# High parts of operand sums moved from GpSimd to ScalarE in an attention and expert kernel

## The chip, the cores and the metric

The kernel runs on one core of one Trainium2 chip. The metric is the device time of one execution in microseconds (us), the median over several runs. The core has five engines that work from instruction streams of their own, each strictly in its own order: TensorE (PE) multiplies matrices, VectorE (DVE), ScalarE (ACT) and GpSimd (POOL) work elementwise, and SyncE (SP) issues the transfers between the chip's memory (DRAM) and the on-chip buffer (SBUF). They wait for each other by semaphores. Matrix products land in PSUM, of which this kernel uses banks of 128 x 512 numbers.

## The reference

First a causal attention with a decay bias over 32 heads of 576 positions and head size 64, then a layer of 4 experts on all 2304 tokens, weighted by given probabilities:

```python
scores = scale * np.matmul(q, k.transpose(0, 1, 3, 2))
cum = np.cumsum(np.maximum(s, 0.0), axis=-1)
bias = -(cum[:, :, :, None] - cum[:, :, None, :])
scores = np.where(causal, -1000000000.0, scores + np.minimum(bias, 0.0))
attn = softmax(scores)                       # rows sum to 1 (+1e-9)
x = np.matmul(attn, v)                       # then reshaped to 2304 x 512
p = domain_probs / (domain_probs.sum(-1, keepdims=True) + 1e-09)
for e in range(4):                           # w1: 512 x 1024, w2: 1024 x 512
    out += p[:, e:e + 1] * (np.maximum(x @ w1[e], 0.0) @ w2[e])
```

## The kernel before

Every factor of a product is held as two numbers, a high part (the value rounded to fp32r) and a low part (the value less its high part). A product is the sum of three matrix products: high by high, high by low, low by high.

**Two stages.** A planner (class `Sched`) orders the attention and, between its steps, a part of expert 0. It ends at some 280 us. What is left of expert 0 is written out in program order (the list `prog`), in groups of token tiles. Three groups are left: group 4 (tiles 10 and 11, 256 columns), group 5 (tiles 12 to 14, 384 columns) and group 6 (tiles 15 to 17, 384 columns). Each has a first layer (L942: `mo` or `pb` from `xg` and `w1h`, `w1l`), whose PSUM results ScalarE turns into the high part of the ReLU (L945, into `hT0`) and VectorE into the low part (L948, into `hT1`); and a second layer (L957), four output rows `dt` of 24 or, in groups 5 and 6, 12 matmuls each. A row `dt` takes first the high parts `hT0`, then the low parts `hT1`, then `hT0` again with `w2l`. VectorE multiplies its result by the token's probability into the sum `acc` (L1212). A group's input tile `xg` is a single buffer: it can be fetched (L932) only when the first layer of the group before is through. Groups 5 and 6 take 48 matmuls for each layer.

From some 372 us on the other experts (and half of expert 0's hidden units) are computed by 2 x 2 block products in seven instead of eight multiplications (`first_layer`, `second_layer`, all matmuls at L1288). That needs sums and differences of blocks of the operands.

**The sums.** The tokens form three pairs of blocks, worked on in the order 1, 2, 0. For each pair `sums_of` makes four operands, called 5, 7, 6 and 3, each 128 x 768: a sum or difference on GpSimd (L1063), its high part on GpSimd (L465), its low part on GpSimd (L450). They are stored to DRAM (`xs_d`, L1096) from a ring of seven buffers (`x`). Pairs 1 and 2 start from single sums fetched from `xf_d` (L1079); pair 0 fetches the high and low parts (L1052) and first joins them on GpSimd (four additions, L1063), and its operands also stay in SBUF.

**The weights' sums.** VectorE makes sums of the blocks of `w1` (four additions of 128 x 512 from SBUF to SBUF, L1063, tiles `t2`, `w1r`, `t`) and of `w2` (four more, tiles `hx`, `w2r`); then ScalarE makes high parts and VectorE low parts of them (L450, tiles `w1l`, `w2l`).

**Fetching back.** The results of groups 0 to 2 were stored to `o_d` in the attention. `back` (L1199) fetches them into `acc`, in 20 transfers.

**What sets the order.** All of that is placed between the matmuls of `prog` by a table: each step has a due time, and after each matmul the steps are written out whose due time is at most `spent`, the sum of the matmuls' planned times. Due times only set the order of the instructions on each engine; nothing starts by the clock. On SyncE each transfer waits besides for the one issued eight before it.

Of the kernel before, what the change touches and what calls it, by code (L numbers as in the profile page):

```python
# [33 lines left out]
HALVES = [(e, s) for e in range(1, E) for s in range(2)] + [(0, 0)]  # L34
LONE = len(HALVES) - 1
LG = 2
SUM_AT = {1: ((0.3, 0.6, 0.9, 1.2), 2.0, 13.5), 2: ((6.0, 6.5, 16.0, 18.0), 23.0, 32.0), 0: ((31.0, 31.5, 32.0, 36.0), 42.0, 57.0)}
T_RAW = (20.0, 25.0)
T_W1 = 42.0
T_W2 = 50.0  # L40
T_BACK = 48.0
START = {7: "4"}
EARLY = {1: "1", 6: "s5", 5: "s7", 7: "2", 3: "s6", 4: "4"}
REST = {1: "6 5", 6: "s3 7", 5: "3"}
ALL = {1: "1", 2: "2", 6: "6", 5: "5", 7: "7"}
# [287 lines left out]
def body(ctx, tc, qk, qkv0, vp, s, dp, w1, w1s, w2, w2s, out):  # L333
# [115 lines left out]
    def sub(e, out, in0, in1):  # L449
        (nc.gpsimd if e == "POOL" else nc.vector).tensor_tensor(out=out, in0=in0, in1=in1, op=ALU.subtract)  # L450
# [572 lines left out]
    xpool = ctx.enter_context(tc.tile_pool(name="xring", bufs=7))  # L1023
    tpool = ctx.enter_context(tc.tile_pool(name="temps", bufs=6))
    spool = ctx.enter_context(tc.tile_pool(name="stage", bufs=1))
    acc = [[mpool.tile([P, TG], F32, name=f"acc{dt}_{b_}") for b_ in range(NT // TG)] for dt in range(KD)]

    def blocks_of(n0, n1):
        return [(b_, max(n0, TG * b_), min(n1, TG * b_ + TG)) for b_ in range(NT // TG) if max(n0, TG * b_) < min(n1, TG * b_ + TG)]
# [10 lines left out]
    def x_tile():  # L1040
        return xpool.tile([P, 2, 2, TG], F32R, tag="x", name="x")

    def temp():
        return tpool.tile([P, 2, TG], F32, tag="t", name="t")

    def flat4(t):
        return t.rearrange("p l k n -> p (l k) n").bitcast(F32)

    def load_block(t, g, i, j):

        n0 = PAIRS[g][i][0] * P
        nc.sync.dma_start(out=flat4(t), in_=xrd[j, :, :, n0:n0 + TG])  # L1052
# [9 lines left out]
    def add(e, out, in0, in1, op):  # L1062
        (nc.gpsimd if e == "POOL" else nc.vector).tensor_tensor(out=out, in0=in0, in1=in1, op=op)  # L1063

    def sums_of(g, held):

        raw, blocks = {}, {}  # L1070
        order = ((1, 0), (1, 1), (0, 0), (0, 1))

        def load(part):
            if held is not None and not held:
                held.update({o: x_tile() for o in (3, 4, 1, 2, 5, 7, 6)})
            for i, j in part:
                if held is None:
                    raw[i, j] = temp()
                    nc.sync.dma_start(out=raw[i, j], in_=xfr[g][j, :, :, TG * i:TG * i + TG])  # L1079
                else:  # L1080
                    t = held[{(0, 0): 1, (0, 1): 2, (1, 1): 4, (1, 0): 3}[i, j]]
                    load_block(t, g, i, j)
                    blocks[i, j] = t

        def join(i, j):
            raw[i, j] = temp()
            add("POOL", raw[i, j], blocks[i, j][:, 0].bitcast(F32), blocks[i, j][:, 1].bitcast(F32), ALU.add)

        def split(o, d, a_, b_, op):
            add("POOL", raw[d], raw[a_], raw[b_], op)  # L1090
            blocks[o] = held[o] if held is not None else x_tile()
            hi("POOL", blocks[o][:, 0], raw[d])
            sub("POOL", blocks[o][:, 1], raw[d], blocks[o][:, 0].bitcast(F32))

        def store(o):
            nc.sync.dma_start(out=xsv[g, SUMS[o]], in_=flat4(blocks[o]))  # L1096

        loads, now, out_at = SUM_AT[g]
        for at, part in zip(loads, order):
            yield at, lambda part=part: load((part,))  # L1100
        if held is not None:
            for i, j in order:
                yield now, lambda i=i, j=j: join(i, j)
                now += 1.9
        for o, d, a_, b_, op in ((5, (1, 1), (1, 0), (1, 1), ALU.add), (7, (1, 0), (0, 0), (1, 0), ALU.subtract),
                                 (6, (0, 0), (1, 1), (0, 0), ALU.subtract), (3, (0, 1), (0, 1), (0, 0), ALU.subtract)):
            yield now, lambda o=o, d=d, a_=a_, b_=b_, op=op: split(o, d, a_, b_, op)
            yield max(now, out_at), lambda o=o: store(o)
            now += 4.7
            out_at += 4.7  # L1110
# [105 lines left out]
    held = {}  # L1216
# [16 lines left out]
    for i, x in enumerate(prog):
        if x[0] == "load":
            if x[2].done is None:
                load_x(x[1], x[3])
        elif x[0] == "l1":
            if x[4].done is None:
                l1_mm(x[1], x[2], bank(x[5]), x[3], x[3] + UN)
                spent += UN * t_pe(x[2]) / 1e3  # L1240
        elif x[0] == "l1e":
            if x[3].done is None:
                l1_hi(x[1], x[2], bank(x[5]))
            if x[4].done is None:
                l1_lo(x[1], x[2], bank(x[5]))
        elif x[0] == "l2":
            if x[3].done is None:
                l2_mm(x[1], x[5], bank(x[4]), x[2], x[2] + UN, x[6])
                spent += UN * t_pe(x[5]) / 1e3
        else:  # L1250
            gi, dt = x[1]
            n0, n1 = GROUPS0[gi][0] * P, GROUPS0[gi][-1] * P + P
            if x[2].done is None:
                evict0(gi, dt, bank(x[4]))
            else:
                if x[3].done is None:
                    nc.sync.dma_start(out=o_d[dt * P:(dt + 1) * P, n0:n1], in_=tok["osb", x[1]][:, 0:n1 - n0])
                assert None not in spilled
                spilled.append((dt, n0, n1))
        if x[0] in ("l1", "l2"):  # L1260
            while steps and steps[0][0] <= spent:
                steps.pop(0)[3]()
        if i == last_l1:
            assert len(w1_first) == len(w2_first) == 3
            wsteps = w1_first
        if i >= last_l1 and wsteps and x[0] in ("l1e", "l2e"):
            for _ in range(3):
                if wsteps:
                    wsteps.pop(0)()
# [251 lines left out]
```

## Time and profile before

| quantity | value |
|---|---|
| median of 3 runs | 934.11 us (932.44 to 936.62) |
| the profiled execution | 933.43 us, span 931.7 us |
| PE busy | 911.6 us, 98% of the span |
| DVE busy | 704.3 us, 76% |
| POOL busy | 516.4 us, 55% |
| ACT busy | 491.9 us, 53% |
| DMA queue of SyncE | 67.1% of 16 engines' span |

PE is busy in nine tenths or more of each of the 40 slices of the page, save the fifteenth (326 to 349 us) and the last; the granted clock is below full in the fifteenth and sixteenth (326 to 373 us):

```profile
PE   9999999999999959999999999999999999999998
PEclk9999999999999988999999999999999999999999
```

So a time is read by asking where PE does not work, or works at a lower clock, and what it waits for there. Transfers issued by SyncE stand as SPq. An instruction's line number is that of the code above.

### The profile page before, as it was taken

Reading aid. Unit: us, or ns where it says so; the run is one execution under the profiler, and the core shown is the slowest. Engines: PE = TensorE matmul, PEld = TensorE weight load, DVE = VectorE, ACT = ScalarE, POOL = GpSimd, SP = SyncE. Lnnn points to the kernel's source line nnn. Section 1 sums busy time; section 2 is a strip of 40 time slices with the busy share of each in tenths; the row PEclk is TensorE's granted clock in tenths of the full one; section 3 lists DMA queues with packets and bytes.
Section 4 is the critical chain, followed back from the end, with each engine's and each line's share of the span. In section 5 each row is a group of like instructions: output and inputs, shape, how many; then the busy total and the mean of one; then the engine's idle time right before and its main releaser. Section 6 shows DMA issues by size and latency. Waiting matters only on the chain.

```text
span 931.7 us, 16516 instructions
## 1 busy us (share of the span) xinstructions
PE 911.6 (98%) x5566; PEld 882.4 (95%) x5566; DVE 704.3 (76%) x1599; ACT 491.9 (53%) x1117; POOL 516.4 (55%) x540
## 2 busy tenths in 40 slices
PE   9999999999999959999999999999999999999998
PEld 7789999899999958999999999999999999999998
DVE  7878888887861546687787878788778886788786
ACT  6898999998860111424443344353344424443343
POOL 4688887887735975017541644353447236541755
PEclk9999999999999988999999999999999999999999
DMA  6788888878517985987766587657864677667101
GB/s 166 190 251 244 229 226 226 237 204 254 169 57 243 376 282 186 312 304 254 231 208 219 196 299 226 206 174 248 299 220 157 223 254 255 217 197 253 61 26 68
DMA packets 132239, 201.34 MB, mean 216 GB/s; under 512 B 11496, under 2 KB 107820, under 8 KB 132156
## 3 DMA queue, kind: packets, MB, share of 16 engines
q1 hardware_dynamic: 132156, 200.30, 67.1%
q8 instruction: 44, 0.72, 0.3%
q14 instruction: 39, 0.32, 0.1%
HBM read 157.34 MB, written 29.05 MB: 200 GB/s over the span
## 4 chain that ended last, share of the span: by engine, by line
PE 88%; DVE 4%; ACT 2%; DMA 2%; SPq 2%; issue 1%; POOL 1%; ACTq 0%; POOLq 0%; DVEq 0%
PE pb L1288 49%; PE mo L1288 8%; PE mo L942 7%; PE mo L957 5%; PE pv L841 5%; PE T L791 3%; PE S L745 3%; PE S L742 2%; PE pb L957 1%; PE pb L942 1%; PE X L791 1%; DMA xs_d<-x 1%; SPq L1199 1%; ACT a L764 1%; DMA xg<-x_d 1%
## 5 line engine op out<-in xcount | busy, mean ns | idle before, releaser
L1288 PE MATMUL pb<-x,w1h 128*128 128x384 f32 x1064 | 270.7, 335 | 0.0
L1288 PEld LDWEIGHTS pb<-x,w1h 128*128 128x128 f32 x1064 | 191.4, 188 | 2.0 <-ACT t L1321 1.6
L1288 PE MATMUL pb<-x,w1l 128*128 128x384 f32 x532 | 177.8, 334 | 0.0
L1296 ACT ACTIVATE pb<-pb 128x384 f32<-128x384 f32 x112 | 53.1, 475 | 202.5 <-DVE t L1328 112.1
L450 POOL TENSOR_TENSOR hT_r<-t,hT_r 128x768 fp32r<-128x768 f32 x18 | 34.8, 1935 | 176.6 <-PE pb L1288 128.7
L1288 PE MATMUL pb<-hT_r,w2h 128*128 128x384 f32 x432 | 109.6, 334 | 0.0
L1288 PEld LDWEIGHTS pb<-x,w1l 128*128 128x128 f32 x532 | 99.8, 188 | 0.0
L942 PE MATMUL mo<-xg,w1h 128*128 128x384 f32 (+1 forms) x304 | 81.4, 338 | 11.5 <-DMA xg<-x_d 11.5
L463 ACT ACTIVATE hT_r<-t 128x768 fp32r<-128x768 f32 x76 | 64.1, 843 | 47.2 <-PE pb L1288 44.3
L764 ACT ACTIVATE a<-a,mx 128x576 f32<-128x576 f32 (+4 forms) x136 | 81.0, 598 | 13.1 <-DVE mx L756 10.2
L1411 DVE TENSOR_TENSOR acc<-pb,acc 128x384 f32<-128x384 f32 x152 | 78.8, 550 | 10.1 <-ACT pb L1296 6.5
L1288 PEld LDWEIGHTS pb<-hT_r,w2h 128*128 128x128 f32 x432 | 78.0, 188 | 0.0
L458 POOL TENSOR_SCALAR a<-a,sm 128x576 f32<-128x576 f32 (+5 forms) x111 | 60.6, 552 | 28.5 <-DVE sm L772 15.0
L450 DVE TENSOR_TENSOR hT_r<-t,hT_r 128x768 fp32r<-128x768 f32 x58 | 58.8, 1013 | 23.0 <-ACT hT_r L463 22.5
L1288 PE MATMUL pb<-xg,w2h 128*128 128x384 f32 x288 | 73.3, 335 | 1.0 <-ACT pb L1296 1.0
L1288 PE MATMUL pb<-hT_r,w2l 128*128 128x384 f32 x216 | 72.2, 334 | 0.0
L1328 DVE TENSOR_TENSOR t<-pb,t 128x384 f32<-128x384 f32 x78 | 39.8, 552 | 41.9 <-ACT t L1321 29.1
L942 PEld LDWEIGHTS mo<-xg,w1h 128*128 128x128 f32 x304 | 53.9, 197 | 14.1 <-DMA xg<-x_d 12.8
L1063 DVE TENSOR_TENSOR t<-t 128x768 f32<-128x768 f32 (+1 forms) x42 | 63.4, 1517 | 0.1
L450 POOL TENSOR_TENSOR xg<-t,xg 128x768 fp32r<-128x768 f32 x19 | 42.9, 2259 | 35.1 <-ACT xg L463 35.1
L820 DVE TENSOR_TENSOR aTl<-T,aTh 128x256 fp32r<-128x256 f32 (+2 forms) x103 | 51.3, 508 | 4.9 <-ACT aTh L463 3.7
L756 DVE CUSTOM_DVE_ANT_0 a<-S,mask 128x448 f32<-128x448 f32 (+4 forms) x107 | 48.1, 456 | 7.4 <-PE S L742 5.8
(245 smaller groups left out, 2335.5 us busy)
## 6 DMA issues: line engine op xcount, KB each, us to landing
x<-xs_d SPq DMA_DIRECT2D x68, 768.0 KB
x<-x_d SPq DMA_DIRECT2D x55, 768.0 KB
xs_d<-x SPq DMA_DIRECT2D x12, 768.0 KB
osb<-p_d SPq DMA_DIRECT2D x19, 384.0 KB
w1r<-in_w1s_dram SPq DMA_DIRECT2D x7, 1024.0 KB
w2r<-in_w2s_dram SPq DMA_DIRECT2D x7, 1024.0 KB
KK<-AB_r SPq DMA_DIRECT2D x24, 288.0 KB
xg<-x_d SPq DMA_DIRECT2D x16, 384.0 KB
```

What stands on the lines that cost most here:

```text
L450: (nc.gpsimd if e == "POOL" else nc.vector).tensor_tensor(out=out, in0=in0, in1=in1, op=ALU.subtract)
L458: (nc.gpsimd if e == "POOL" else nc.vector).tensor_scalar(out, in_, scale, 1.0 if bias is None else bias, op0=ALU.mult, op1=ALU.mult if bi ...
L463: nc.scalar.activation(out, in_, AF.Copy)
L756: nc.vector.tensor_tensor_reduce(out=z[0:n, j0:j1], in0=tok["S", (c, pi)][0:n, 0:j1 - j0], in1=mask[0:n, 448 - a + j0:448 - a + j1], scale ...
L764: nc.scalar.activation(z[0:n, 0:bb], z[0:n, 0:bb], AF.Exp, bias=tok["mx", c][0:n, k:k + 1], scale=-1.0, accum_out=tok["sm", c][0:n])
L820: nc.vector.tensor_tensor(out=dst, in0=src, in1=h_.bitcast(F32), op=ALU.subtract)
L942: nc.tensor.matmul(t[:, 0:w], wl[q][:, dc, o:o + P], xgt[:, l, dc, 0:w], start=(u == 0), stop=(u == 3 * KD - 1))
L957: nc.tensor.matmul(t[:, 0:w], wl[fc // 2][:, fc % 2, 128 * dt:128 * dt + 128], ht[:, fc, 0:w], start=(u == 0), stop=(u == 3 * len(fcs) - 1))
L1063: (nc.gpsimd if e == "POOL" else nc.vector).tensor_tensor(out=out, in0=in0, in1=in1, op=op)
L1288: nc.tensor.matmul(ts[u], wv[wl][:, k, 128 * u:128 * u + 128], x[xl_][:, k, :], start=start and k == 0 and n == 0, stop=k == 1 and n == 2, ...
L1296: nc.scalar.activation(out[u], in_[u], AF.Copy)
L1411: nc.vector.tensor_tensor(out=d, in0=ts[u], in1=d, op=ALU.add)
```

## The change

The constants that set the order change; in `sums_of` the three steps of an operand (sum, high, low) become separate steps with due times of their own, and the high part is made by ScalarE instead of GpSimd; the ring's buffers are taken with the fetches; the fetches of `xg` become steps with a due time 2.5 after their place; `back` fetches all four `dt` of a block at once (5 transfers instead of 20) and is due at 21 instead of 48; `acc` becomes one tile for each block of tokens; the steps that sum the weights are due at 32 and 37 instead of 36 and 50; in the table `FIRST` one operand's step moves by one product.

```diff
-SUM_AT = {1: ((0.3, 0.6, 0.9, 1.2), 2.0, 13.5), 2: ((6.0, 6.5, 16.0, 18.0), 23.0, 32.0), 0: ((31.0, 31.5, 32.0, 36.0), 42.0, 57.0)}
-T_RAW = (20.0, 25.0)
+SUM_AT = {1: ((0.3, 0.6, 0.9, 1.2), 15.0), 2: ((6.0, 6.5, 25.0, 25.5), 30.0), 0: ((33.0, 36.0, 38.5, 43.0), 45.0)}
+T_RAW = (20.0, 28.0)
-T_BACK = 48.0
+T_SUMS = (32.0, 37.0)
+T_BACK = 21.0
+T_XG = 2.5
-FIRST = {1: "s5 s7 1", 6: "s6 6", 5: "2 s3", 4: "5", 3: "7 3"}
+FIRST = {1: "s5 s7 1", 6: "s6 6", 5: "2 s3", 3: "5 7 3"}
...
-    acc = [[mpool.tile([P, TG], F32, name=f"acc{dt}_{b_}") for b_ in range(NT // TG)] for dt in range(KD)]
+    acct = [mpool.tile([P, KD, TG], F32, name=f"acc{b_}") for b_ in range(NT // TG)]
+    acc = [[t[:, dt] for t in acct] for dt in range(KD)]
...
-        def split(o, d, a_, b_, op):
+        def total(o):
+            d, a_, b_, op = sums[o]
             add("POOL", raw[d], raw[a_], raw[b_], op)
-            blocks[o] = held[o] if held is not None else x_tile()
-            hi("POOL", blocks[o][:, 0], raw[d])
-            sub("POOL", blocks[o][:, 1], raw[d], blocks[o][:, 0].bitcast(F32))
+
+        def high(o):
+            hi("ACT", outs[o][:, 0], raw[sums[o][0]])
+
+        def low(o):
+            sub("POOL", outs[o][:, 1], raw[sums[o][0]], outs[o][:, 0].bitcast(F32))
...
+        for at, f, o in ((0.0, total, 5), (0.0, total, 7), (2.6, high, 5), (2.6, low, 5), (2.6, total, 6), (4.6, high, 7), (4.6, low, 7),
+                         (4.6, total, 3), (8.6, high, 6), (8.6, low, 6), (12.4, high, 3), (12.4, low, 3),
+                         (8.5, store, 5), (12.0, store, 7), (15.7, store, 6), (18.0, store, 3)):
+            yield now + at, lambda f=f, o=o: f(o)
...
-        for dt, n0, n1 in spilled:
+        for n0, n1 in sorted({x[1:] for x in spilled}):
...
-                nc.sync.dma_start(out=acc[dt][b_][:, u0 - TG * b_:u1 - TG * b_], in_=o_d[dt * P:(dt + 1) * P, u0:u1])
+                nc.sync.dma_start(out=acct[b_][:, 0:len(ds), u0 - TG * b_:u1 - TG * b_],
+                                  in_=o_d[0:P * len(ds), u0:u1].rearrange("(d p) n -> p d n", p=P))
...
-    steps.append((T_W1 - 6.0, 9, 0, lambda: w_begin(1, w1_first)))
+    steps.append((T_SUMS[0], 9, 0, lambda: w_begin(1, w1_first)))
...
-    steps.append((T_W2, 9, 0, lambda: w_begin(2, w2_first)))
+    steps.append((T_SUMS[1], 9, 0, lambda: w_begin(2, w2_first)))
...
         if x[0] == "load":
             if x[2].done is None:
-                load_x(x[1], x[3])
+                steps.append((spent + T_XG, -1, x[3], lambda x=x: load_x(x[1], x[3])))
+                steps.sort(key=lambda x: x[:3])
```

How the instructions stand before and after is seen in three places. The first is VectorE, from the first product of group 4's second layer on (`acc` from `mo_102`); `t`, `w1r` are sums of `w1`, `hx`, `w2r` sums of `w2`. Before:

```order
L1212 TENSOR_TENSOR acc_3_3940<-mo_102,osb 128x256
L1212 TENSOR_TENSOR acc_3_3946<-mo_103,osb 128x256
L1063 TENSOR_TENSOR t_4330<-w1r 128x512
L1063 TENSOR_TENSOR w1r<-w1r 128x512
L1063 TENSOR_TENSOR t<-w1r,t_4330 128x512
L1063 TENSOR_TENSOR t<-w1r,t 128x512
L1212 TENSOR_TENSOR acc_3_3952<-pb_3965,osb 128x256
L1212 TENSOR_TENSOR acc_3_3958<-pb_3966,osb 128x256
L948 SCALAR_TENSOR_TENSOR hT_r<-pb_3967,hT_r 128x384
L450 TENSOR_TENSOR w1l_80<-w1r,w1h_76 128x512 x2
L948 SCALAR_TENSOR_TENSOR hT_r<-pb_3968,hT_r 128x384
L450 TENSOR_TENSOR w1l_81<-t,w1h_77 128x512
```

And with the change:

```order
L1224 TENSOR_TENSOR acc_3940<-mo_102,osb 128x256
L1066 TENSOR_TENSOR t_4264<-w1r 128x512
L1066 TENSOR_TENSOR w1r<-w1r 128x512
L1066 TENSOR_TENSOR t<-w1r,t_4264 128x512
L1066 TENSOR_TENSOR t<-w1r,t 128x512
L1224 TENSOR_TENSOR acc_3940<-mo_103,osb 128x256
L1066 TENSOR_TENSOR hx_f<-w2r 128x512
L1066 TENSOR_TENSOR w2r<-w2r 128x512
L1066 TENSOR_TENSOR hx_f<-hx_f,w2r 128x512
L1066 TENSOR_TENSOR hx_f<-w2r,hx_f 128x512
L1224 TENSOR_TENSOR acc_3940<-pb_3947,osb 128x256
L1224 TENSOR_TENSOR acc_3940<-pb_3948,osb 128x256
```

The four sums of `w1` now stand ahead of the second product of group 4 (`mo_103`), and the four sums of `w2`, which stood behind group 5's last low part, stand ahead of the third and fourth (`pb_3947`, `pb_3948`). All eight are thus ahead of the low parts of group 5's ReLU, which stand behind these rows, in the same order as before among the `w1l`.

The second place is SyncE's queue around the fetch of group 6's input (`xg`, 384 columns). Before, behind the stores of pair 2:

```order
L1199 DMA acc_1_3950<-o_d 128x256
L1199 DMA acc_2_3951<-o_d 128x128
L1199 DMA acc_1_3956<-o_d 128x256
L1199 DMA acc_2_3957<-o_d 128x128
L932 DMA xg<-x_d 128x2x384 x4
L1033 DMA osb<-p_d 128x384
L1096 DMA xs_d<-x 128x4x384 x3
L1033 DMA osb<-p_d 128x384
L1096 DMA xs_d<-x 128x4x384
```

And with the change:

```order
L1055 DMA x<-x_d 128x4x384
L1103 DMA xs_d<-x 128x4x384
L1055 DMA x<-x_d 128x4x384 x2
L1103 DMA xs_d<-x 128x4x384 x2
L1055 DMA x<-x_d 128x4x384
L1103 DMA xs_d<-x 128x4x384 x2
L1036 DMA osb<-p_d 128x384
L934 DMA xg<-x_d 128x2x384 x4
L1103 DMA xs_d<-x 128x4x384 x2
L1036 DMA osb<-p_d 128x384
L1103 DMA xs_d<-x 128x4x384 x2
```

The fetches of `acc` are gone from here (they stand, five in number, ahead of the first store). Ahead of `xg` stand the last stores of pair 2, mixed with the fetches of pair 0, and the fetch of probabilities `osb`.

The third place is ScalarE from group 4's sixth ReLU on; names carry buffer numbers here, `hT0_r_593` is written by the ReLUs and `w1h` from `w1r` and `t`. Before:

```order
L945 ACTIVATE hT0_r_593<-pb1_3966 128x256
L945 ACTIVATE hT0_r_593<-pb2_3967 128x256
L945 ACTIVATE hT0_r_593<-pb3_3968 128x256
L945 ACTIVATE hT0_r_593<-pb2_3967 128x384
L463 ACTIVATE w1h0_76<-w1r_4149 128x512 x2
L945 ACTIVATE hT0_r_593<-pb3_3968 128x384
L463 ACTIVATE w1h1_77<-t_4332 128x512
L945 ACTIVATE hT0_r_593<-mo_0_102 128x384
```

And with the change, where `x_3960` is the high part of pair 1's operand 3, and `x_4010` to `x_4013` are those of pair 2's operands 5, 7, 6 and 3:

```order
L947 ACTIVATE hT0_r_593<-pb1_3948 128x256
L947 ACTIVATE hT0_r_593<-pb2_3949 128x256
L465 ACTIVATE x_3960<-t_3972 128x768
L947 ACTIVATE hT0_r_593<-pb3_3950 128x256
L465 ACTIVATE x_4010<-t_4019 128x768
L465 ACTIVATE x_4011<-t_4014 128x768
L465 ACTIVATE x_4012<-t_4182 128x768
L947 ACTIVATE hT0_r_593<-pb2_3949 128x384
L465 ACTIVATE w1h0_76<-w1r_4125 128x512
L465 ACTIVATE x_4013<-t_4191 128x768
L465 ACTIVATE w1h0_76<-w1r_4125 128x512
L947 ACTIVATE hT0_r_593<-pb3_3950 128x384
```

High parts that wait for GpSimd's sums now stand between the ReLUs that wait for PE. The one of pair 1's operand 3 stands behind the seventh ReLU of group 4, and the last of pair 2 ahead of group 5's second ReLU.

## Rows read from the trace of the kernel before

**Rows 1.** Busy time of the engines by stretch: start:end, length, then each engine.
```profile
319.73:329.67 9.94, 9.22 (x50) 8.26 (x49) 7.18 (x10) 3.56 (x7) 5.80 (x4) 1.00 1.07 384
329.67:338.57 8.90, 8.78 (x49) 8.14 (x48) 6.81 (x5) 2.68 (x5) 7.50 (x4) 1.00 0.85 298
338.57:349.25 10.68, 0.01 (x2) 0.01 (x1) 0.00 (x0) 0.00 (x0) 10.42 (x8) 0.60 0.77 228
349.25:362.36 13.11, 12.27 (x48) 11.34 (x49) 8.35 (x8) 1.48 (x3) 12.32 (x8) 0.67 0.81 274
362.36:371.87 9.51, 9.35 (x50) 8.44 (x50) 5.44 (x11) 2.05 (x4) 0.00 (x0) 1.00 0.23 83
```

**Rows 2.** Chain that ended last: start, length, engine, tile, line, instructions.
```profile
280.22 8.32 PE mo L957 x48
```

**Rows 3.** SyncE's DMA queue in order of time: start, length, line, transfer, count.
```profile
323.50 11.42 SPq L1096 DMA_DIRECT2D xs_d<-x  x3
334.97 10.40 SPq L1199 DMA_DIRECT2D acc<-o_d  x20
345.47 1.91 SPq L932 DMA_DIRECT2D xg<-x_d  x4
```

**Rows 4.** TensorE in order of time: start, length, operands, count, idle before.
```profile
329.67 1.95 PE L957 MATMUL pb<-hT_r,w2h 128*128 128x384 f32 x8
349.25 1.01 PE L942 MATMUL mo<-xg,w1h 128*128 128x384 f32 x2 [10.67 <-DMA xg<-x_d]
353.48 1.01 PE L942 MATMUL mo<-xg,w1h 128*128 128x384 f32 x2 [0.84 <-DMA xg<-x_d]
```

**Rows 5.** Granted TensorE clock in stretches of 2 us (the fourth number, PEclk).
```profile
342.00:344.00 2.00, 0.00 (x0) 0.50 0.67 178
356.00:358.00 2.00, 2.00 (x8) 0.53 0.93 338
358.00:360.00 2.00, 2.00 (x14) 1.00 0.82 285
```

**Rows 6.** GpSimd in order of time, the second and third pair's sums.
```profile
313.14 1.85 POOL L1063 TENSOR_TENSOR t<-t 128x768 f32<-128x768 f32 x1
315.08 1.16 POOL L465 TENSOR_SCALAR x<-t 128x768 fp32r<-128x768 f32 x1
316.32 2.16 POOL L450 TENSOR_TENSOR x<-t,x 128x768 fp32r<-128x768 f32 x1
318.44 2.29 POOL L1063 TENSOR_TENSOR t<-t 128x768 f32<-128x768 f32 x1
330.98 1.32 POOL L465 TENSOR_SCALAR x<-t 128x768 fp32r<-128x768 f32 x1 [5.29 <-DMA xs_d<-x]
```

**Rows 7.** VectorE in order of time, 311 to 330 us.
```profile
311.29 0.42 DVE L1212 TENSOR_TENSOR acc<-mo,osb 128x256 f32<-128x256 f32 x1 [1.98 <-PE mo L957]
314.51 1.03 DVE L1063 TENSOR_TENSOR t<-w1r 128x512 f32<-128x512 f32 x1
315.57 1.20 DVE L1063 TENSOR_TENSOR w1r<-w1r 128x512 f32<-128x512 f32 x1
316.69 4.58 DVE L1063 TENSOR_TENSOR t<-w1r,t 128x512 f32<-128x512 f32 x2
321.20 0.74 DVE L1212 TENSOR_TENSOR acc<-pb,osb 128x256 f32<-128x256 f32 x2
326.77 0.55 DVE L948 SCALAR_TENSOR_TENSOR hT_r<-pb,hT_r 128x384 fp32r<-128x384 f32 x1
328.89 0.69 DVE L450 TENSOR_TENSOR w1l<-w1r,w1h 128x512 fp32r<-128x512 f32 x1
```

**Rows 8.** ScalarE in order of time: a ReLU, and a high part of 768.
```profile
307.03 0.39 ACT L945 ACTIVATE hT_r<-pb 128x256 fp32r<-128x256 f32 x1 [1.12 <-PE pb L942]
394.01 0.83 ACT L463 ACTIVATE hT_r<-t 128x768 fp32r<-128x768 f32 x1
```

**Rows 9.** Chain that ended last: the landing of a store of sums.
```profile
319.17 11.66 DMA xs_d<-x
```

More of the change, by code (lines that the diff above doesn't have):

```diff
@@ L1065, in sums_of, with load @@
     def sums_of(g, held):
-        raw, blocks = {}, {}
+        raw = {}
         order = ((1, 0), (1, 1), (0, 0), (0, 1))
[L1073 to L1083, printed above, removed]
+        def load(i, j):
+            if not outs:
+                outs.update({o: x_tile() for o in ((5, 7, 6, 3) if held is None else (3, 4, 1, 2, 5, 7, 6))})
+                if held is not None:
+                    held.update(outs)
+            if held is None:
+                raw[i, j] = temp()
+                nc.sync.dma_start(out=raw[i, j], in_=xfr[g][j, :, :, TG * i:TG * i + TG])
+            else:
+                load_block(outs[whole[i, j]], g, i, j)
@@ L1085, in join @@
         def join(i, j):
             raw[i, j] = temp()
-            add("POOL", raw[i, j], blocks[i, j][:, 0].bitcast(F32), blocks[i, j][:, 1].bitcast(F32), ALU.add)
-        def split(o, d, a_, b_, op):
+            t = outs[whole[i, j]]
+            add("POOL", raw[i, j], t[:, 0].bitcast(F32), t[:, 1].bitcast(F32), ALU.add)
+        def total(o):
+            d, a_, b_, op = sums[o]
             add("POOL", raw[d], raw[a_], raw[b_], op)
-            blocks[o] = held[o] if held is not None else x_tile()
-            hi("POOL", blocks[o][:, 0], raw[d])
-            sub("POOL", blocks[o][:, 1], raw[d], blocks[o][:, 0].bitcast(F32))
+        def high(o):
+            hi("ACT", outs[o][:, 0], raw[sums[o][0]])
@@ L1095, in store @@
+        def low(o):
+            sub("POOL", outs[o][:, 1], raw[sums[o][0]], outs[o][:, 0].bitcast(F32))
         def store(o):
[L1096 to L1100, printed above, removed]
-        if held is not None:
[L1102 to L1110, printed above, removed]
+            nc.sync.dma_start(out=xsv[g, SUMS[o]], in_=flat4(outs[o]))
@@ new lines, in sums_of @@
+        outs = {}
+        whole = {(0, 0): 1, (0, 1): 2, (1, 1): 4, (1, 0): 3}
+        sums = {5: ((1, 1), (1, 0), (1, 1), ALU.add), 7: ((1, 0), (0, 0), (1, 0), ALU.subtract),
+                6: ((0, 0), (1, 1), (0, 0), ALU.subtract), 3: ((0, 1), (0, 1), (0, 0), ALU.subtract)}
+        loads, now = SUM_AT[g]
+        for at, (i, j) in zip(loads, order):
+            yield at, lambda i=i, j=j: load(i, j)
+        if held is not None:
+            for k, (i, j) in enumerate(order):
+                yield now + 1.9 * k, lambda i=i, j=j: join(i, j)
+            now += 7.6
@@ L1196, in back @@
     def back():
-        for dt, n0, n1 in spilled:
+        for n0, n1 in sorted({x[1:] for x in spilled}):
+            ds = [dt for dt, *x in spilled if x == [n0, n1]]
+            assert ds == list(range(len(ds)))
             for b_, u0, u1 in blocks_of(n0, n1):
-                nc.sync.dma_start(out=acc[dt][b_][:, u0 - TG * b_:u1 - TG * b_], in_=o_d[dt * P:(dt + 1) * P, u0:u1])
+                nc.sync.dma_start(out=acct[b_][:, 0:len(ds), u0 - TG * b_:u1 - TG * b_],
+                                  in_=o_d[0:P * len(ds), u0:u1].rearrange("(d p) n -> p d n", p=P))
         spilled.append(None)
```

## The prediction

> **What bounds the kernel now.** I read the page's slices first: PE is busy nearly everywhere, so only a stretch in which it waits can give time back. Cutting that stretch at the ends of layers [rows 1] shows groups 5 and 6. Each of the four layers has 48 matmuls, which take 8.32 us where nothing disturbs them [rows 2], so four take 33.3; from 319.73 to 371.87 they take 52.14. The loss of 18.9 us is the most that the change can give in this stretch: 9.94 - 8.32 = 1.6 in group 5's first layer, 8.90 - 8.32 = 0.6 in its second, 10.7 idle, 13.11 - 8.32 = 4.8 in group 6's first, 1.2 in its second [rows 1]. Then the queue and PE in order of time: PE waits 10.67 us for group 6's `xg` [rows 4], and SyncE reaches that fetch at 345.47 only, because three stores that wait for GpSimd hold it for 11.42 us and the 20 fetches of `acc` for 10.40 more [rows 3]. Last the clock: it stands at 0.50 within the idle time, is at 0.53 in the 2 us before 358 and at 1.00 after [rows 5]. Of the 4.8 us in group 6's first layer 0.84 is a second wait [rows 4]; the rest, 3.95, I put down to that lower level (1.2 instead of 2.4 GHz).
>
> **The queue's part.** With `acc` fetched earlier and in five pieces, 10.40 us leave SyncE's queue ahead of `xg`. The five come ahead of the first store, where SyncE has to wait for GpSimd. One piece is not in the trace: between 0.48 us (1.91 for four `xg`) and 3.8 (11.42 for three stores, waits included) [rows 3]; I take 0.52, the mean of the old ones, 2.6 in all. At 19 us, the upper end, the cover would be used up but `xg` of group 5 still waits for PE to free its buffer at about 308.
>
> What is left ahead of group 6's `xg` are pair 2's last stores. They need pair 2's last low part. GpSimd now runs eight additions for a pair, without the four high parts (0.83 us for one on ScalarE, [rows 8]). But it starts pair 2 no earlier: ScalarE makes pair 1's last high part only behind group 4's seventh ReLU (307.03 + 0.39, [rows 8]), which PE's progress fixes, so the high part ends at 308.3 and the low part, 1.85 us [rows 6], at 310.1. From there pair 2's eight additions take 8 x 1.85 = 14.8 alone and 8 x 2.29 = 18.3 beside VectorE (below), and end at 325 to 328.5. The old pause of 5.29 us, in which GpSimd waited for a buffer [rows 6], goes. So `xg` is issued once group 5's first layer frees it, at 328 to 331, and lands within the 11.66 us that the slowest store in this stretch took [rows 9], by 342. For the queue alone, PE would lose 0 to 4 us there instead of 10.7.
>
> **What is late next: VectorE.** The eight sums of the weights now stand ahead of two results of group 4, and of the low parts of group 5's ReLU. Such a sum from SBUF to SBUF takes 0.69 us at 328.89, in GpSimd's pause before 330.98 [rows 6, 7]. While GpSimd works it is another thing. GpSimd's instructions end at 314.99, 316.24, 318.48 and 320.73 [rows 6]; the four sums of `w1` end at 315.54, 316.77, 318.98 (the mean of the two) and 321.27 [rows 7]. Each ends 0.50 to 0.55 us after a GpSimd instruction, and the next GpSimd instruction ends later by as much. So the two take turns, one sum for one addition; where GpSimd only adds, a turn is 4.58 / 2 = 2.29 us. Instructions that read PSUM are not held up: a low part takes 0.55, a pair of results 0.74 [rows 7].
>
> The rule behind it is in the Trainium skill, SBUF — State Buffer, section "Who interferes with whom": a VectorE instruction with two SBUF inputs and a GpSimd instruction that reads SBUF exclude each other, and the second one waits until the first is through. By that rule a sum would end its full 0.69 after GpSimd's end; the trace shows 0.50 to 0.55. With 0.69 the twelve turns below would be 0.15 to 0.2 longer each and the forecast some 2 us higher; I go by the row.
>
> Now the turns, with GpSimd busy without a pause (pair 2's eight additions, then pair 0's joins):
> - VectorE is through with group 4's first result at 311.29 + 0.42 = 311.7 [rows 7]. GpSimd's first addition of pair 2 ends at 312.0, the first sum of `w1` at 312.5.
> - Seven more turns for the other seven sums: 312.5 + 7 x 2.29 = 328.5. (The second result of group 4 stands among them and costs no turn.)
> - The last two results of group 4: 0.74, 329.2. Group 5's second layer, ready at 319.73 + 8.32 = 328.05, needs the first of these banks.
> - First low part 0.55, then two `w1l` (turns 9 and 10, 330.8 and 333.1), second low part 333.6, `w1l` 335.4, third 335.9, `w1l` 337.7, fourth low part 338.2.
>
> PE has done four matmuls with high parts by then, and one for each low part that came. From the last low part on, 137 are left: 5 of this row, 36 of the other three, 96 of group 6. At 8.32 / 48 they take 23.75 us. PE was all but idle for 8 us, so I charge the lower clock as the trace shows it after 10.67 us idle, 3.95, and 0.6 for group 6's second layer, as group 5's lost (its first eight matmuls took 1.95, [rows 4]). End: 338.2 + 23.75 + 3.95 + 0.6 = 366.5, against 371.87. Group 6's `xg` (by 342) is then no longer waited for, since group 5 ends at about 348.
>
> **The rest at nothing.** The second stage gets the same instructions; pair 0's sums, with twelve additions and some four turns behind 328.5, end near 355, ahead of its first use after 366. The step moved in `FIRST` is one high and one low part that VectorE has 6 us to make (three products of 12 matmuls) before their product. The tile `acc` in another shape moves no work. A waiting high part on ScalarE holds up the ReLUs behind it: pair 2's last one follows a sum that ends at about 323.5, the ReLU behind it is ready at 323.9 (half of group 5's first layer), so about 1 us, hidden behind VectorE.
>
> **Sum.** 371.87 - 366.5 = 5.4 us less. The profiled execution took 933.43 (span 931.7), so 928.0; the median of the runs shown is 0.7 above it, 928.7 from there. I take 928.4. The forecast's own range: with the lower clock not granted at all 924.5; with one turn more (2.29) and 0.8 us more behind ScalarE 931.5.
>
> **Rivals.**
> A. The eight sums fit in. If GpSimd pauses in pair 2 (a high part that comes late, a buffer not yet free), sums run in 0.69 instead of 2.29, and all twelve end by about 321 and the low parts with their ReLUs. Then PE runs 319.73 + 33.3 + 0.6 = 353.6 plus 0 to 4 for `xg`: 14 to 18 us less, 916 to 920; with some turns left 922. For it: GpSimd now depends on ScalarE for each low part, and paused 5.29 us in this place before. Against: by the sums above every high part is ready before its turn.
> B. ScalarE holds PE. The high part of pair 2's operand 3 needs the buffer of a store issued at about 312; the slowest landing was 11.66 us [rows 9], so 324, with no room left. Each us after that moves three of group 5's ReLUs; landing at T, the last low part comes at about T + 4, which passes 338.2 at T = 334, and the gain is gone at 339.5: 934. Against: twice the slowest landing.
> C. The clock stays low. At 0.50 each of the 137 matmuls costs 0.173 more. The sum holds 3.95, some 23 of them. If new waits break PE's work (group 6's results and low parts behind `w2l`, which take turns with pair 0 too) and the level stays, the gain is used up after 54 matmuls, it is slower by 0.5% after about 81, and at all 137 the end is 338.2 + 47.5 + 0.6 = 386.3: 948. For it: a thin PE for 10 us. Against: after 349.25 continuous work brought full clock back in 8.7 us [rows 4, 5], and after 338.2 I find no wait.
>
> **How the numbers follow.** Forecast 0.55, A 0.25, B 0.12, C 0.08. A measurement tells about 0.5% from no change, 4.7 us. Faster means below 929.4: A and two thirds of the forecast, 0.62; same: the rest of the forecast and B, 0.30; slower: C, 0.08. The range of 916.5 to 934 leaves out C, some of B and the fastest of A. The likeliest one's own is 924.5 to 931.5.
>
> **What would show it.** Right: PE's long wait moves from group 6's first layer to group 5's second, released by VectorE's L948 line (its number moves), near 330 to 338; the eight sums take about 2.3 us each; no PE wait for `xg` over 1 us in group 6; half clock after the wait. The queue's step is wrong if `xg` is still waited for; VectorE's if the sums take 0.7; the clock's if it stays at 1.00. The forecast is wrong if group 5's second layer runs through, or if PE waits on ScalarE's ReLUs.

## The result, and the profile after

The changed kernel takes 924.57 us (median; 924.12 to 925.64), the kernel before 933.53 beside it (932.44 to 936.62): ratio 0.990, 95% interval 0.9875 to 0.9926. That is 9.0 us less; the forecast was 928.4, 5.7 below the 934.11 shown then. The profiled execution took 924.77, its span is 923.0 against 931.7.

The stretch that was to change, cut at the ends of the layers, is set out as in [rows 1] (start:end, length, then busy time and count of PE, its weight loads, DVE, ACT and POOL, the clock, DMA share and GB/s). The four lines are the two layers of group 5 and the two of group 6:

```profile
319.97:329.13 9.16, 8.89 (x51) 8.26 (x49) 9.09 (x8) 3.87 (x8) 7.59 (x5) 1.00 1.06 391
329.13:345.36 16.23, 11.00 (x49) 9.56 (x49) 8.64 (x9) 4.46 (x8) 13.40 (x7) 0.79 0.89 300
345.36:355.28 9.92, 9.23 (x49) 8.28 (x49) 9.14 (x10) 2.25 (x5) 9.38 (x5) 1.00 0.62 203
355.28:363.93 8.65, 8.59 (x49) 8.27 (x49) 4.00 (x7) 2.79 (x5) 1.84 (x1) 1.00 0.50 182
```

From the start of group 5 to that of the second stage it is 363.93 - 319.97 = 44.0 us, where it was 52.0. ([Rows 1] has 52.1, because it cuts the second stage at 371.87; in the trace before its first matmul starts at 371.71.) PE's long pause between groups 5 and 6 [rows 4] is gone; group 5's second layer has become the slow one, 16.23 us for 8.32 of work. PE in order of time (idle time before, and what ended it, in brackets) and PE's waits (total, times, longest) show where:

```profile
332.36 0.44 PE L959 MATMUL pb<-hT_r,w2h 128*128 128x384 f32 x1 [1.82 <-DVE hT_r L950]
...
336.79 0.69 PE L959 MATMUL pb<-hT_r,w2h 128*128 128x384 f32 x1 [1.53 <-DVE hT_r L950]
...
348.41 0.62 PE L944 MATMUL mo<-xg,w1h 128*128 128x384 f32 x2 [0.25 <-DMA xg<-x_d]
```

```profile
PE pb L959 <- DVE hT_r L950: 5.1, 3, 1.8
PE mo L944 <- DMA xg<-x_d: 0.7, 3, 0.2
```

The three waits before the low parts (1.82, 1.77 and 1.53, together 5.1) are new; the last ends at 336.79. Group 6 starts as soon as group 5 is through (345.36 above), then waits three times for a further piece of `xg`, the last time until 348.41. The clock around the end of the waits (fourth number, as in [rows 5]):

```profile
336.00:338.00 2.00, 1.22 (x4) 0.50 1.02 378
338.00:340.00 2.00, 2.00 (x9) 0.56 1.06 399
```

It is at 0.50 at the end of the waits, and back at 1.00 about 3 us after the last one (0.56 from 338 to 340 means full speed for the last 0.24 us, so from 339.8 on). VectorE, in order of time, as in [rows 7]:

```profile
312.70 2.22 DVE L1066 TENSOR_TENSOR w1r<-w1r 128x512 f32<-128x512 f32 x1
314.84 4.59 DVE L1066 TENSOR_TENSOR t<-w1r,t 128x512 f32<-128x512 f32 x2
...
326.22 0.69 DVE L1066 TENSOR_TENSOR hx_f<-w2r,hx_f 128x512 f32<-128x512 f32 x1
...
336.19 0.54 DVE L950 SCALAR_TENSOR_TENSOR hT_r<-mo,hT_r 128x384 fp32r<-128x384 f32 x1
```

Behind the first (0.79, as forecast) the sums take 2.0 to 2.3 us each, except the last, at 326.22, which takes 0.69. It fell into a pause of GpSimd (as in [rows 6]):

```profile
323.34 2.29 POOL L452 TENSOR_TENSOR x<-t,x 128x768 fp32r<-128x768 f32 x1
327.20 1.85 POOL L452 TENSOR_TENSOR x<-t,x 128x768 fp32r<-128x768 f32 x1 [1.57 <-ACT x L465]
```

SyncE's queue, as in [rows 3]; `x<-x_d` is a piece of pair 0, fetched into a buffer of the ring:

```profile
294.19 7.32 SPq L1210 DMA_DIRECT2D acc<-o_d  x5
...
320.90 3.82 SPq L1103 DMA_DIRECT2D xs_d<-x  x2
332.15 0.36 SPq L1055 DMA_DIRECT2D x<-x_d  x1
...
335.01 3.92 SPq L934 DMA_DIRECT2D xg<-x_d  x4
```

Behind the two stores SyncE does nothing until 332.15. Its waits (total, times, longest) name the cause, the buffer whose old contents are still being stored:

```profile
SPq L1055 <- DMA xs_d<-x: 7.3, 1, 7.3
```

The rule that a transfer waits for the one eight before it does not explain this wait: that one was a piece of group 5's `xg`, which PE was using by 322.3.

So `xg` of group 6 is issued at 335.01, 10.5 us earlier than before and four to seven later than the forecast had it.

### The profile page after: what moved, and what is told of

The parts are those of the page before. It is cut to its first block, busy times and chain, and to the rows that moved or that the text cites. A ratio compares the mean times of both kernels' runs of the same rounds, so it can differ in the third digit from the quotient of the medians.

```text
span 923.0 us, 16496 instructions
## 1 busy us (share of the span) xinstructions
PE 909.8 (99%) x5566; PEld 880.6 (95%) x5566; DVE 710.9 (77%) x1599; ACT 501.3 (54%) x1129; POOL 509.5 (55%) x528
## 4 chain that ended last, share of the span: by engine, by line
PE 85%; DVE 7%; ACT 4%; DMA 1%; issue 1%; POOL 1%; SPq 0%; ACTq 0%; POOLq 0%; DVEq 0%
PE pb L1301 49%; PE mo L1301 9%; PE mo L944 6%; PE mo L959 5%; PE pv L843 4%; PE T L793 3%; PE S L747 2%; PE pb L959 1%; PE S L744 1%; PE pb L944 1%; ACT a L766 1%; PE X L793 1%; DMA xg<-x_d 1%; DVE t L1066 1%; DVE w1l L452 1%
## 5 line engine op out<-in xcount | busy, mean ns | idle before, releaser
L944 PE MATMUL mo<-xg,w1h 128*128 128x384 f32 (+1 forms) x304 | 78.8, 328 | 0.7 <-DMA xg<-x_d 0.7
L944 PEld LDWEIGHTS mo<-xg,w1h 128*128 128x128 f32 x304 | 51.9, 190 | 3.2 <-DMA xg<-x_d 1.6
```

The costliest lines, as they stand in the source:

```text
L944: nc.tensor.matmul(t[:, 0:w], wl[q][:, dc, o:o + P], xgt[:, l, dc, 0:w], start=(u == 0), stop=(u == 3 * KD - 1))
```

## The experiments

Each kernel ran with the kernel before on the same chip (before: 932.6 to 933.8 in all of them). A row of the form "PE tile line <- engine tile line: total, times, longest" is from the view of PE's waits, 280 to 372 us; each kernel has its own line numbers. Rows are of the one profiled execution of a kernel, times the median of its runs.

### Single parts

**The sums of the weights alone**, in the kernel before:

```diff
-    steps.append((T_W1 - 6.0, 9, 0, lambda: w_begin(1, w1_first)))
+    steps.append((32.0, 9, 0, lambda: w_begin(1, w1_first)))
...
-    steps.append((T_W2, 9, 0, lambda: w_begin(2, w2_first)))
+    steps.append((37.0, 9, 0, lambda: w_begin(2, w2_first)))
```

> The kernel before with only the weights' eight sums moved (due at 32 and 37). Theory (turns with GpSimd; the moved sums delay group 5's low parts): PE waits 3 to 7 us for VectorE in group 5's second layer, which it does not in the kernel before, but group 6's input is issued at 345.5 as before, so this wait lies in the time in which PE waited for it anyway: 931 to 936, no gain. Rival (the sums' place gave a part of the gain): 927 to 930.

Measured: 932.97 us, ratio 1.000 (0.9989 to 1.0012). PE's waits, and the queue's `xg` row:

```profile
PE mo L942 <- DMA xg<-x_d: 9.2, 3, 8.2
PE pb L957 <- DVE hT_r L948: 1.3, 2, 0.8
```

```profile
345.01 1.92 SPq L932 DMA_DIRECT2D xg<-x_d  x4
```

No gain, and none could come: `xg` is issued where it was [rows 3]. VectorE's wait was smaller than I expected (1.3 against 3 to 7).

**The spilled results alone**, in five pieces and due at 21, in the kernel before:

```diff
-T_BACK = 48.0
+T_BACK = 21.0
...
-    acc = [[mpool.tile([P, TG], F32, name=f"acc{dt}_{b_}") for b_ in range(NT // TG)] for dt in range(KD)]
+    acct = [mpool.tile([P, KD, TG], F32, name=f"acc{b_}") for b_ in range(NT // TG)]
+    acc = [[t[:, dt] for t in acct] for dt in range(KD)]
...
-                nc.sync.dma_start(out=acc[dt][b_][:, u0 - TG * b_:u1 - TG * b_], in_=o_d[dt * P:(dt + 1) * P, u0:u1])
+                nc.sync.dma_start(out=acct[b_][:, 0:len(ds), u0 - TG * b_:u1 - TG * b_],
+                                  in_=o_d[0:P * len(ds), u0:u1].rearrange("(d p) n -> p d n", p=P))
```

> The kernel before with only the part that fetches spilled results in five pieces and at 21 instead of 48. Theory 1: SyncE reaches group 6's input at 335 instead of 345.5 (behind pair 2's last low part at 334.5), it lands near 341.5, PE waits some 3 us from 338.6 instead of 10.7, the clock stays up or falls for 1 to 2 us only: 933.5 less 9 to 12, so 921.5 to 924.5, as much as the whole change gave. Rival (the transfers, not the queue, are the limit, since they are busy all the time there): the fetch lands 4 to 6 us later than that and the gain is 3 to 6 us, 927.5 to 930.5. Rival 2: the gain of the change came from the high parts on ScalarE; then this gives under 2 us.

Measured: 928.4 us, 0.9954 (0.9938 to 0.9971). About half of the change's gain: less than I expected, and inside the 927.5 to 930.5 of the first rival. The waits and `xg` of group 6:

```profile
PE pb L942 <- DMA xg<-x_d: 4.6, 2, 4.3
PE mo L942 <- DMA xg<-x_d: 1.6, 4, 0.9
```

```profile
302.70 8.39 SPq L1202 DMA_DIRECT2D acc<-o_d  x5
...
314.60 4.22 SPq L932 DMA_DIRECT2D xg<-x_d  x4
...
339.11 2.78 SPq L932 DMA_DIRECT2D xg<-x_d  x4
```

`xg` is issued 6.4 us earlier than before and 4.1 later than in the changed kernel; the three stores ahead of it still wait for GpSimd. The 4.3 us are new: `xg` of group 5, issued at 314.60, now comes behind the five pieces of `acc`. In the changed kernel these are issued from 294.19 on, that `xg` at 307.81, and PE waits 0.2 us for it.

**`FIRST` as before**, all else changed:

```diff
-FIRST = {1: "s5 s7 1", 6: "s6 6", 5: "2 s3", 3: "5 7 3"}
+FIRST = {1: "s5 s7 1", 6: "s6 6", 5: "2 s3", 4: "5", 3: "7 3"}
```

> The changed kernel with the table FIRST as before: operand 5 is made one product earlier. Theory: the wait of 1.00 us for ScalarE's copy of a PSUM bank, which PE had at 404 us in the kernel before and has no longer, comes back in the same place (some 396 us), and the time rises by 1 us, to about 925.6. Rival: that wait went because the stage before shifted; then no wait in the second stage and no difference.

Measured: 924.69 us, 0.9921 (0.9902 to 0.9941). The wait (here of the second stage, 390 to 420 us) is back:

```profile
PE pb L1301 <- ACT pb L1309: 1.0, 1, 1.0
```

The row shows the mechanism. In the profiled execution the second stage takes 559.8 us, 0.8 more than in the changed kernel, but the part ahead of it is 0.7 shorter; 0.1 us between the medians is too little to tell the gain.

**High parts on GpSimd**, all else changed:

```diff
-            hi("ACT", outs[o][:, 0], raw[sums[o][0]])
+            hi("POOL", outs[o][:, 0], raw[sums[o][0]])
```

> The changed kernel with the high parts made by GpSimd again, everything else (order, queue, fetches) as changed. Theory (the stage is bound by VectorE's turns and by SyncE's wait for a store's landing, not by GpSimd's own work): GpSimd works without its waits for ScalarE, pair 2's last low part comes within 2 us of the changed kernel's 329.0, the sums beside a GpSimd high part take some 1.2 instead of 2.3 us, group 6's input lands within 2 us of 345 to 348, time 923.5 to 926.5. Rival (the high parts on ScalarE are what gave the gain): twelve times 0.9 us more on GpSimd end in PE's waits, 928 to 932.

Measured: 923.35 us (922.84 to 928.31), 0.9916 (0.9889 to 0.9943), not slower than with ScalarE. A high part on GpSimd with the VectorE sum beside it, and PE's wait for VectorE:

```profile
311.88 1.27 POOL L467 TENSOR_SCALAR x<-t 128x768 fp32r<-128x768 f32 x1
312.49 1.20 DVE L1066 TENSOR_TENSOR w1r<-w1r 128x512 f32<-128x512 f32 x1
```

```profile
PE pb L959 <- DVE hT_r L950: 3.1, 2, 1.7
```

Beside a high part on GpSimd a sum takes 1.20 us, not 2.22: GpSimd's list is longer, but VectorE is through earlier, and PE waits 3.1 us for it, not 5.1.

### The two ends that meet

**The sums of `w2` later**: VectorE is relieved, the transfers are left alone.

```diff
-T_SUMS = (32.0, 37.0)
+T_SUMS = (32.0, 50.0)
```

> The changed kernel with one number undone: the four sums of w2 are due at 50 again instead of 37, so they stand behind group 5's low parts. Theory 1 (VectorE and GpSimd take turns, but since the change the fetch of group 6's input is issued only at 335.0 to 338.9 us, because SyncE waits for the landing of a store before it, and lands at 345.4 to 348.4): the last low part comes about 2 us earlier (some 334.5 instead of 336.7), PE's three waits for VectorE shrink to 1 to 4 us in all, but PE then waits for group 6's input instead, and the time stays within 2 us of 924.6. Theory 2 (VectorE's eight sums alone bound the stage, the input is hidden): the time falls by the 2 to 4 us that the low parts come earlier, to 920.5 to 922.5.

Measured: 923.76 us, 0.9906 (0.9891 to 0.9921).

```profile
PE pb L959 <- DVE hT_r L950: 3.4, 2, 1.8
PE mo L944 <- DMA xg<-x_d: 2.0, 1, 2.0
```

VectorE's waits are 1.7 us shorter than the 5.1 of the change, and the wait for group 6's `xg` is 1.3 longer than the 0.7 there: what the one gives up the other mostly takes, as the first theory had it.

**The low parts of `w1` later**: they no longer stand between the low parts of the ReLU.

```diff
-T_W1 = 42.0
+T_W1 = 48.5
```

> The changed kernel with the low parts of w1's first four blocks due at 48.5 and later instead of 42, so that group 5's four low parts of the ReLU stand together ahead of them on VectorE. Theory 1 (group 6's input is the second bound, at 345.4 to 348.4 us): PE's waits for VectorE in group 5's second layer go (5.1 us now), that layer ends near 338.5, and PE then waits 7 to 10 us for group 6's input, with the clock falling to half: 924 to 929, no gain. Theory 2 (VectorE alone bounds the stage): group 6 starts at 338.5 instead of 345.4, time 917 to 919.

Measured: 926.44 us, 0.9933 (0.9916 to 0.9949): slower than the change, and far from the 917 to 919 of the second theory.

```profile
345.48 1.01 PE L944 MATMUL mo<-xg,w1h 128*128 128x384 f32 x2 [7.90 <-DMA xg<-x_d]
```

```profile
PE pb L959 <- DVE hT_r L950: 0.7, 1, 0.7
```

```profile
348.00:350.00 2.00, 2.00 (x10) 0.69 0.45 156
```

Group 6 starts when its input is there, at 345.48, no earlier than the 345.36 of the changed kernel. What is lost besides is mostly the clock: it is at 0.50 until 349.2 and again from 359.5 to 362.9.

**The spilled results behind group 6's `xg`**: the transfers are relieved, VectorE is left alone.

```diff
-T_BACK = 21.0
+T_BACK = 56.0
```

> One edit to the changed kernel: the fetch of the spilled results (1.84 MB) comes behind group 6's xg in SyncE's queue, not ahead of group 5's. Theory 1 (these bytes stand in the transfers ahead of both xg, but VectorE's low part of group 5 at 336.7 is the bound of nearly the same end): group 6's xg is issued at 328 to 333 in place of 335.0, the 0.7 us for which TensorE waits for it go, the wait for VectorE (9.9 us in three) stays, 923.3 to 924.3. Theory 2 (the transfers alone are the limit): the gain is that of several microseconds of transfer, 920 to 922.5. Theory 3 (the bytes have long landed by then and cost nothing): 924.0 to 925.0, xg at 335 and its waits as before.

Measured: 924.55 us, 0.9906 (0.989 to 0.9922). (The 9.9 us in the expectation is a slip of mine; the three waits add up to 5.1.) PE's waits, and the clock:

```profile
PE pb L959 <- DVE hT_r L950: 6.4, 3, 3.3
```

```profile
342.00:344.00 2.00, 2.00 (x9) 0.63 1.10 357
```

The time is that of the third theory, but by other rows than it named. The three runs together show what bounds the changed kernel. Almost without VectorE's waits PE meets `xg` and waits 7.9 us for it (second run); with `xg` there in time no wait for it is left (third), and the time stays. In the third GpSimd no longer pauses, so the eighth sum of VectorE takes 2.22, the last low part ends at 337.68, 0.95 later, the clock comes back at 343.5 instead of 339.8, and group 6 starts at 347.59. So two chains end close to each other, the transfers at 345.5 and VectorE's at 345.4, and relieving one leaves the other; that VectorE's ends still later in the third run goes with the pause that GpSimd no longer makes there.

### Towards a better version

**`w1`'s low parts late, and a fetch of pair 0 behind `xg`**: the one on which SyncE had waited.

```diff
-SUM_AT = {1: ((0.3, 0.6, 0.9, 1.2), 15.0), 2: ((6.0, 6.5, 25.0, 25.5), 30.0), 0: ((33.0, 36.0, 38.5, 43.0), 45.0)}
+SUM_AT = {1: ((0.3, 0.6, 0.9, 1.2), 15.0), 2: ((6.0, 6.5, 25.0, 25.5), 30.0), 0: ((33.0, 36.0, 38.5, 51.0), 45.4)}
...
-T_W1 = 42.0
+T_W1 = 48.5
```

> As the kernel with the low parts of w1 late, and the fourth fetch of pair 0, for which SyncE waits 7.3 us until a store has landed, is moved behind the fetch of group 6's input. Theory 1: SyncE reaches that fetch at about 330 instead of 335, it lands at 336 to 341, PE waits 0 to 3 us for it and neither waits for VectorE nor loses the clock: 917 to 921. Theory 2 (the queue is not what holds that fetch, or the transfers are slow anyway): as the kernel without this move, within 1 us.

Measured: 926.65 us, 0.9932 (0.9917 to 0.9947); a miss. The wait has moved to ScalarE, and GpSimd (second fence) shows why:

```profile
PE pb L959 <- ACT hT_r L947: 5.1, 2, 3.2
```

```profile
344.37 1.83 POOL L1066 TENSOR_TENSOR t<-x 128x768 f32<-128x768 f32 x1 [10.18 <-DMA x<-x_d]
```

The fourth join waits 10.18 us for the late fetch; behind it stand the totals, behind these the high parts on ScalarE, and behind them the ReLUs of group 6.

**The same with the fourth join late too** (due 45.0), behind the three totals that do not need it:

```diff
-                yield now + 1.9 * k, lambda i=i, j=j: join(i, j)
+                yield now + (1.9 * k if k < 3 else 11.6), lambda i=i, j=j: join(i, j)
```

> The changed kernel with three moves of order: w1's low parts behind group 5's low parts, pair 0's fourth fetch behind group 6's input, and its join behind pair 0's other sums (the version with the first two had ScalarE's ReLUs of group 6 wait 5.1 us behind high parts whose sums stood behind that join, which waited 10.2 us for its fetch). Theory: neither VectorE nor the input nor ScalarE holds PE for more than 2 us in all, the clock stays at full, the second stage begins at 357 to 359.5 instead of 363.9: 918 to 920.5. Rival (VectorE's eight w1 and w2 low parts in turns with GpSimd now hold group 6's low parts): PE waits 3 to 5 us in group 6's second layer, 921 to 924.

Measured: 922.43 us (919.64 to 923.17), 0.9888 (0.9864 to 0.9911); the lowest median so far, though 2 us above what I expected.

```profile
PE mo L944 <- DMA xg<-x_d: 1.6, 2, 1.3
PE pb L944 <- DMA xg<-x_d: 1.3, 1, 1.3
```

ScalarE's wait is gone; waits for `xg` of both groups are left, and 0.7 us for VectorE. The expectation that the clock stays at full failed too: it is at 0.50 from 342.5 to 345.9.

**That, and the spilled results behind `xg`** (`T_BACK = 56.0`):

> The version with late w1 low parts and a late fourth join, with the fetch of the spilled results behind group 6's xg as well. That version's trace has TensorE waiting 1.34 us for group 5's xg, 1.6 us for group 6's xg and 0.7 us for VectorE. Theory 1 (the 1.84 MB of spilled results delay both xg): the 2.9 us for xg go, 919.0 to 921.0. Rival (the stores ahead of xg are what delays it): the waits for xg stay, 922 to 923.5.

Measured: 923.82 us (921.24 to 923.92), 0.989 (0.9872 to 0.9907); expected 919 to 921. The waits, the clock behind them, and two low parts of the weights on VectorE:

```profile
PE pb L959 <- DVE hT_r L950: 4.2, 1, 4.2
PE mo L944 <- DMA xg<-x_d: 0.2, 1, 0.2
```

```profile
354.00:356.00 2.00, 2.00 (x8) 0.50 0.98 349
```

```profile
340.77 1.87 DVE L452 TENSOR_TENSOR w1l<-t,w1h 128x512 fp32r<-128x512 f32 x1
...
349.75 1.82 DVE L452 TENSOR_TENSOR w2l<-hx_f,w2h 128x512 fp32r<-128x512 f32 x1
```

The waits for `xg` went as expected. But with the fetches early GpSimd adds without a pause from 327.5 on (in the version before it had paused 2.02 us at 344.3, and two of VectorE's low parts took 0.68), so from 336 on each low part of a weight takes 1.8 to 2.3 us, and those of group 6's ReLU come late behind them: PE stands still for 4.2 us, and the clock falls to 0.50 (351.9 to 358.8).

**That, and the high parts on GpSimd** (`hi("POOL", ...)` as above):

> The same as the last, with the high parts of the operand sums on GpSimd again, behind each total. Theory (a high part on GpSimd holds a VectorE sum 1.2 us and not 2.3, and spares the waits between GpSimd and ScalarE): the last low part of group 5 comes earlier than in the last version, VectorE's wait of 0.7 us goes, 918.0 to 920.5. Rival (GpSimd's longer list makes joins and stores late, and the fetches of x behind them): 921 to 924, with a wait for xg or for ScalarE's high parts.

Measured: 918.01 us (917.83 to 919.13), 0.9838 (0.9821 to 0.9856). It beats the changed kernel by some 6.6 us (the two intervals of the ratio do not meet) and the last version, on the same chip, by 5.8. The same two instructions, PE's wait, the clock and the start of the second stage:

```profile
339.13 0.84 DVE L452 TENSOR_TENSOR w1l<-t,w1h 128x512 fp32r<-128x512 f32 x1
...
347.11 0.84 DVE L452 TENSOR_TENSOR w2l<-hx_f,w2h 128x512 fp32r<-128x512 f32 x1
```

```profile
PE pb L959 <- DVE hT_r L950: 1.4, 1, 1.4
```

```profile
350.00:352.00 2.00, 2.00 (x12) 1.00 0.74 258
```

```profile
357.09 0.51 PE L1301 MATMUL pb<-x,w1h 128*128 128x384 f32 x2
```

They take 0.84 where a high part of GpSimd lies beside them. The wait for VectorE, which I had expected to go, is 1.4 us, 2.8 less than in the last version, and the clock stays at 1.00. The second stage starts 6.0 us earlier than in that version (363.13): 0.8 lie ahead of group 6's second layer, 2.8 are the shorter wait, and 2.4 come behind it, where the clock had been at 0.50. From group 5 on, the 52.0 us of the kernel before have become 357.09 - 319.85 = 37.2, of which 33.3 are work.

## Why the prediction was right, and where it was not

**What bounds, and where the wait goes.** Right: the pause for `xg` went, and the wait moved to the low parts of group 5's ReLU on VectorE. The sums at 32 and 37 are no gain by themselves: alone they bring nothing, and with `w2`'s sums later again the changed kernel is not slower.

**The queue's part.** This step failed. I had said that only pair 2's last stores are left ahead of group 6's `xg`, and that it is issued once group 5's first layer frees it, at 328 to 331. A fetch of pair 0 stands there too, as the order of the queue showed, and I did not ask what its ring buffer waits for: 7.3 us for a store. Issue came at 335.01, and the last piece landed some 6 us after the 342 I had set. What this costs without VectorE's waits the run with `w1`'s low parts late shows, 7.9 us and not my 0 to 4; in the changed kernel it costs 9.92 - 8.32 = 1.6, because VectorE holds PE at the same time. By my sign, no wait for `xg` over 1 us, the step would pass: the waits in the profile add up to 0.7. The five pieces of `acc` took 7.32 on the queue, not 2.6, but were hidden, as forecast (PE waits 0.2 us for group 5's `xg`).

**VectorE's turns.** Right: sums of 2.0 to 2.3 us, GpSimd's additions of 2.28 to 2.30. (The 0.69 at 328.89 in [rows 7] that the forecast calls a sum is a low part of a weight, of the same shape; the sum at 326.22 takes as long.) The end of the last low part, forecast 338.2, was 336.73; the difference is the one sum that met GpSimd's pause (0.69, not 2.29). The pause came by rival B's mechanism, a high part on ScalarE that waits for a store's landing:

```profile
326.28 0.85 ACT L465 ACTIVATE x<-t 128x768 fp32r<-128x768 f32 x1 [2.20 <-DMA xs_d<-x]
```

**The clock.** Right in kind, mis-sized: charged 3.95, measured 1.46 (from 336.79 to 345.36 there are 41 matmuls, 7.11 us at full clock, in 8.57). The 3.95 came from one case, the stop of 10.67 us, behind which the low level lasted 8.6 us more; here it lasted 3.0, and behind another full stop, of 7.90 us, 3.8 (the run with `w1`'s low parts late). One case was too few to size it.

**The sum, by its own terms.** Forecast 338.2 + 23.75 + 3.95 + 0.6 = 366.5. Measured 336.79 + 23.75 + 1.46 (clock) + 1.60 (`xg`) + 0.33 (group 6's second layer, 8.65 - 8.32) = 363.93. So of the 3.3 us between the spans forecast (926.3, from 931.7 less 5.4) and measured (923.0), 2.5 are the clock and 1.4 the low part; `xg` took 1.6 back, the smaller terms gave 0.3; and 0.76 lie behind it, where the second stage is 0.92 shorter, and 0.16 goes the other way because the forecast started from 371.87 instead of 371.71. That the errors of the clock and of `xg` pull opposite ways is luck.

**The rest at nothing.** Wrong for `FIRST`: the second stage takes 559.1 us instead of 560.0, and the wait of 1.0 us that it lost comes back with the old table. I had asked only whether the moved step could be late, not whether the old place had a wait.

**The rivals.** A did not come, one sum excepted. B came as a 2.2 us wait on ScalarE behind VectorE's, and at full size, 5.1 us on PE, where a fetch was moved behind `xg`. C did not come.

**The title's part.** The high parts on ScalarE, by themselves, brought nothing that I could measure, and in the last two versions, which differ in them alone, they cost 5.8 us (923.82 against 918.01). The spilled results alone bring half of the 9 us. The other half comes with the new order of sums, stores and fetches as a whole. One part of it the rows show, the 4.3 us for group 5's `xg` that the changed kernel does not have; no run took it apart further.

By the Trainium skill, SBUF — State Buffer, section "Who interferes with whom", a VectorE instruction with two inputs in SBUF and a GpSimd instruction that reads SBUF shut each other out. The trace agrees that they hold each other up, but not that they do so in full. A high part on GpSimd alone takes 0.83 in the kernel before:

```profile
301.09 0.83 POOL L465 TENSOR_SCALAR x<-t 128x768 fp32r<-128x768 f32 x1
```

By a full exclusion a sum that has to let a high part through would take 0.83 + 0.69 = 1.52 (an estimate from rows: the two alone); the run with the high parts on GpSimd has 1.20, so the two overlap in part. The fastest version draws on the same: with GpSimd's list cut into shorter pieces (a high part of 1.27 among additions of 2.29), two of VectorE's low parts of the weights go from 1.8 to 0.84.

## What to carry to other kernels

When one wait is taken away, look up at once what ends next, and on which queue: here VectorE and the transfers ended almost together, so relieving either alone gave 0.8 us, nothing, or a loss of 1.9; relieving both, and keeping GpSimd out of VectorE's way, gave 6.6. Of a transfer that is to come earlier, check every one issued ahead of it for what its own buffer waits for, not only for its length. And where VectorE and GpSimd take turns, an engine that is "freed" of short instructions may hold the other one longer. And count a stop of PE with the clock that falls with it: in the last two versions 2.8 us of wait came with 2.4 more behind it.

## What the runs showed of the hardware that I had not expected

- A VectorE instruction of 128 x 512 with two inputs in SBUF takes 0.69 us when GpSimd pauses, 1.20 beside a high part (128 x 768, one input), and mostly 2.2 to 2.3 beside additions of 128 x 768. GpSimd's high part itself goes from 0.83 to 1.27.
- The granted clock came back after very different times once a wait had ended: 3.0 us in the changed kernel (336.79 to 339.8), 5.7 in the one with the spilled results behind `xg` (337.74 to 343.5), 3.8 in the one with `w1`'s low parts late (345.48 to 349.2), 6.7 in the last version but one (352.10 to 358.8), and 8.6 in the kernel before (349.25 to about 357.9). In the first two PE had done single matmuls while it waited, in the last three it had stood still, for 7.90, 4.23 and 10.67 us. So neither that nor the length of the stop tells these times apart; what does, no run here shows.
